# Attention, a bilinear layer and a SoLU layer in one kernel: single-bank tiles for the products of h, other room for the first raw words of w_in, a fence behind block 4's first casts

## The chip, the cores and the metric

The kernel runs on one core of one Trainium2 chip. The metric is device microseconds (us) of one execution. The core's engines are PE (TensorE, the matrix products), DVE (VectorE), ACT (ScalarE), POOL (GpSimd) and SP (SyncE, which here only issues transfers). SBUF is the working memory; PSUM, eight banks of 512 fp32 values per partition, is where PE leaves its products.

## The reference

Three layers follow one another over 2304 tokens (4 x 576) of width 512.

```
x   = repeat(attention over 4-token means) + local attention (|i - j| < 4)   # 8 heads of 64
x   = ((x @ w_a) * (x @ w_b)) @ w_out                                        # 512 -> 1536 -> 512
h   = x @ w_in                                                               # 512 -> 1024
e   = exp(h - max(h));  solu = h * e / (sum(e) + 1e-9)
out = ((solu - mean) / sqrt(var + 1e-6) * g_ln) @ w_out2                     # 1024 -> 512
```

## The kernel before, in words

The values are fp32. A product is made of three PE products of a high and a low part (hi x hi, hi x lo, lo x hi), so each operand is split: ACT casts the high part, DVE or POOL subtracts it to get the low part. The weights arrive as raw 64-bit words; `w_stages` loads one (`load`, L102), has ACT scale its two halves (`s1`, L112 and L113), DVE shift and add them (`s2`, `s3`), ACT cast the high part (`s4`) and DVE or POOL form the low part (`s5`).

**First part.** Attention, and the bilinear layer in blocks of 512 tokens; block 4, the last, has 256. A block goes in 12 chunks j: `emit_A` (L655) makes a and b, `emit_a` copies a out (ACT), `emit_mult` multiplies (DVE, L668), `emit_p` splits the product (ACT ph L674, POOL pl L675), and `emit_B` (L696) adds the chunk to four sums, one or two chunks later. At j = 11 the sums are copied out (o1, L704 and L709) and stored to DRAM. The first weights lie in 36 slots `w0` to `w35`, three for each chunk; a slot is free when its chunk in block 4 is done, and is then used again. `slot(31)` held o1 of block 4.

**Passage.** During block 4 `start_p2` (called at j = 2) closes the attention's pools, opens those of the last stage and lists the work on w_in and w_out2 (16 pieces) in `w2q`, each item with the chunk from which it may be traced. Every raw word goes into the slot that its weight will have, so a load waits for the slot's old weight.

**Last part.** Tokens in 18 tiles of 128. The first four go singly: `emit_C1` multiplies a tile with w_in into h (L815), a tile of two PSUM banks with two buffers, and DVE reduces it to its row maximum (L818). From there the tiles go in pairs p = 2 to 8 through `emit_C` (L835): seven products of 6 matmuls each stand for eight, with sums of operands (S1 to S4, made by POOL in `x_sums`, split by ACT in `x_hi` and by POOL in `x_lo`) and of weights (T1 to T4). Their four targets d, a, b, c are the halves of two such h tiles. ACT copies a to v1 (L845), DVE makes u2 = b + v1 (L848) and u3 = c + u2 (L852), and `top` adds and takes the maximum in one operation (L839); h ends in SBUF, in slots 31 and 34. The order on PE is d, a, b, c, a again, b again, d again.
For each tile follow the SoLU and the norm: `emit_exp` (ACT, L870), `emit_mean` (DVE, L875 and L877), `emit_sq` (ACT), `emit_V` (DVE transposes, then a store), `emit_raw` (loads it back with rows and columns exchanged), `emit_rs` (L888 to L893), `emit_T` (ACT L920, POOL L922), and `emit_D` (L931), 24 matmuls with w_out2; `emit_out` scales and stores. A pair's `emit_D` comes two pairs after its `emit_C`. `x_load` reads a pair's o1 into slots 20 and 23, of which there is one set; `x_hi` of pair 2 casts into slots 26 and 29, `x_lo` of pair 2 fills 32 and 35.

**What sets the order.** The program is written in one order; a planner then orders each engine's instructions, by that order and its own estimates of durations, and puts in the waits. A tile is given on when all its readers are done. `pin` ties an engine's instructions to the order as written: all engines in block 0, PE in blocks 1 and 2, four engines in block 3, all engines from pair 3 on. `pin(())`, in block 4, for the four single tiles and for pair 2, ties nothing.

Of the kernel before, what the change touches and what calls it, by code (L numbers as in the profile page):

```python
# [7 lines left out]
F32 = mybir.dt.float32  # L8
# [34 lines left out]
def kernel(  # L43
# [15 lines left out]
):  # L59
    nc = tc.nc  # L60
    PE, ACT, DVE, POOL, SP = nc.tensor, nc.scalar, nc.vector, nc.gpsimd, nc.sync
    last = {}
    done = [0]

    def pin(engines=None):

        traced = nc.cur_bb.bb.instructions
        for ins in traced[done[0]:]:
            if ins.engine in last and (engines is None or ins.engine in engines):
                tc.add_manual_dep(  # L70
                    ins, last[ins.engine].name,
                    mybir.DependencyInfo(mybir.DependencyClass.NoSync, mybir.DependencyReason.DATA), reason="pin")
            last[ins.engine] = ins
        done[0] = len(traced)
# [19 lines left out]
    def slot(n, dt=F32R, shape=(128, 2, 512), name=None):  # L94
        return base.tile(list(shape), dt, tag=f"w{n}", name=name or f"w{n}")

    def w_stages(src, i, dst, at, gcol=None, lo_eng=DVE, keep=None):


        st = {}  # L100

        def load():  # L102
            raw = slot(at, I32, (128, 1024), "raw")
            SP.dma_start(out=raw, in_=src[i])
            words = raw.rearrange("p (a b) -> p a b", b=2)
            st["low"], st["high"] = words[:, :, 0], words[:, :, 1]

        def s1():


            hw = f32(st["high"])
            ACT.activation(out=hw, in_=hw, func=AF.Prelu, scale=2.0 ** -112, alpha=2.0 ** 32)  # L112
            ACT.activation(out=st["low"], in_=st["low"].bitcast(U32), func=AF.Copy, scale=2.0 ** -29)  # L113

        def s2():
            st["w"] = base.tile([128, 512], I32, tag="wm", bufs=3, name="wm")
            DVE.tensor_scalar(out=st["w"], in0=st["high"], scalar1=3, scalar2=None, op0=ALU.logical_shift_left)

        def s3():
            DVE.tensor_tensor(out=st["w"], in0=st["w"], in1=st["low"], op=ALU.add)  # L120
            if keep is not None:
                keep[i] = f32(st["w"])

        def s4():
            t = slot(at)
            dst[i] = t[:, 0, :], t[:, 1, :]
            if gcol is None:
                ACT.copy(out=dst[i][0], in_=f32(st["w"]))
            else:
                ACT.activation(out=dst[i][0], in_=f32(st["w"]), func=AF.Copy, scale=gcol)  # L130

        def s5():
            hi, lo = dst[i]
# [544 lines left out]
    def emit_B(blk, j):  # L678
        w = width[blk]
        if j == 0:  # L680
            if w == WIDE:
                t = aps.tile([128, 2, 512], F32, tag="S", name="accS")
                accs[blk] = [ps.tile([128, 512], F32, tag=f"acc{n}", name=f"acc{n}") for n in range(2)] + [t[:, n] for n in range(2)]
            else:
                t = [ps.tile([128, 2, 256], F32, tag=f"acc{n}", name=f"acc{n}") for n in range(2)]
                accs[blk] = [t[n // 2][:, n % 2, :] for n in range(4)]
        def store(m):
            SP.dma_start(out=o1d[blk][:, :, 128 * m:128 * m + 128].rearrange("i p t -> p i t"),
                         in_=o1s[blk][:, m, 0:w].rearrange("p (i t) -> p i t", t=128))

        ph, pl = pt.pop((blk, j))
        wh, wl = W1[3 * j + 2]
        for m in range(4):
            ms = slice(m * 128, m * 128 + 128)
            for i, (wt, x) in enumerate(((wh, ph), (wh, pl), (wl, ph))):
                PE.matmul(out=accs[blk][m], lhsT=wt[:, ms], rhs=x,  # L696
                          start=(j == 0 and i == 0 and (w == WIDE or m % 2 == 0)), stop=(j == NCH - 1 and i == 2),
                          skip_group_check=True)
            if j == NCH - 1:
                if m == 0:  # L700
                    o1s[blk] = (base.tile([128, NP, WIDE], F32, tag="xs", name="o1") if w == WIDE else
                                slot(31, F32, (128, NP, 256), "o1"))
                if m < 2 or w < WIDE:
                    ACT.copy(out=o1s[blk][:, m, 0:w], in_=accs[blk][m])  # L704
                    store(m)
        if j == NCH - 1 and w == WIDE:

            for m in (2, 3):
                DVE.tensor_copy(out=o1s[blk][:, m, 0:w], in_=accs[blk][m])  # L709
                store(m)  # L710
# [90 lines left out]

        return first, second, [split(n) for n in range(4)]

    def h_of():
        return p2["ps"].tile([128, FF2], F32, tag="h", bufs=2, name="h")

    def emit_C1(i):
        hi, lo = x1.pop(("t", i))
        h = h_of()
        for n in range(2):  # L810
            for k in range(4):
                wh, wl = W2[2 * k + n]
                ks = slice(k * 128, k * 128 + 128)
                for q_, (x, w) in enumerate(((hi, wh), (hi, wl), (lo, wh))):
                    PE.matmul(out=h[:, n * 512:n * 512 + 512], lhsT=x[:, ks], rhs=w,  # L815
                              start=(k == 0 and q_ == 0), stop=(k == 3 and q_ == 2))
        mx = col("mx")
        DVE.tensor_reduce(out=mx, in_=h, axis=AX.X, op=ALU.max)  # L818
        hst[i] = {"h": h, "mx": mx}

    def emit_C(p):


        ops = x1.pop(p)
        sb = p2["sb"]
        d, a, b, c = (t[:, 512 * n:512 * n + 512] for t in (h_of(), h_of()) for n in range(2))
        i, k = 2 * p, 2 * p + 1

        def prod(out, x, b, more=False):
            xh, xl = ops[x]  # L830
            for kt in range(2):
                wh, wl = WB[b, kt]
                ks = slice(kt * 128, kt * 128 + 128)
                for q_, (xx, w) in enumerate(((xh, wh), (xh, wl), (xl, wh))):
                    PE.matmul(out=out, lhsT=xx[:, ks], rhs=w, start=(kt == 0 and q_ == 0 and not more),  # L835
                              stop=(kt == 1 and q_ == 2), skip_group_check=True)

        def top(out, in0, in1, op, init, mx):
            DVE.tensor_tensor_reduce(out=out, in0=in0, in1=in1, scale=1.0, scalar=init, op0=op, op1=ALU.max, accum_out=mx)  # L839

        hA, hB = (slot(n, F32, (128, FF2), "h") for n in (31, 34))
        prod(d, "S1", "T1")
# [182 lines left out]
    def start_p2():  # L1025
        open_p2()
        load_o1(0)
        load_o1(1)
        stages = [w_stages(w2, i, W2, 3 * (i // 2) + i % 2, g_sb[:, i - 8:i - 7] if i >= 8 else None,
                           POOL if i % 2 else DVE, wk) for i in range(16)]  # L1030
        for n, i in enumerate((0, 1, 5, 4, 2, 3, 7, 6) + tuple(range(8, 16))):
            kt = n // 4
            w2q.append((max(2, n // 2), stages[i][0]))
            body = list(stages[i][1:])
            if n in (2, 6):
                ts = []
                body.insert(3, lambda kt=kt, ts=ts: (ts.extend(t_sums(kt)), ts[0]()))
            if n in (3, 7):
                body.insert(3, lambda ts=ts: ts[1]())
            w2q.extend((min(max(3, n // 2 + 1) + m // 2, 11), f) for m, f in enumerate(body))  # L1040
            if n in (3, 7):
                w2q.extend((7 if kt == 0 else 11.5, lambda ts=ts, q_=q_: ts[2][q_]()) for q_ in range(4))
        w2q.append((11.2, lambda: x_load(2)))
        w2q.sort(key=lambda x: x[0])

# [49 lines left out]
    blk = NBLK - 1  # L1095
    advance(1e9)
    for j in range(NCH):
        if j == 2:
            start_p2()
        for n in range(2):  # L1100
            emit_A(blk, j, n, 0, width[blk])
            (emit_mult if n else emit_a)(blk, j)
        emit_p(blk, j)
        prev.append((blk, j))
        if len(prev) > 2 or j < 1:
            emit_B(*prev.pop(0))
        for t_, f in w2q:
            if j <= t_ < j + 1:
                f()
        if j == 8:  # L1110
            split_o1(0)
            split_o1(1)
            load_o1(2)
            load_o1(3)
        pin(())
    for x in prev:
        emit_B(*x)

# [6 lines left out]
    for i in range(4):  # L1125
        emit_C1(i)
        emit_exp(i)
        emit_mean(i)
        emit_sq(i)
        emit_V(i)  # L1130
        emit_rs(i)
        emit_raw(i)
        if i < 2:
            split_o1(i + 2)
        if i == 1:
            x_sums(2)
            x_hi(2)
            x_lo(2)
            x_load(3)
        if i == 3:  # L1140
            x_sums(3)
            x_hi(3)
            x_lo(3)
        if i == 2:
            emit_D(0)
            emit_out(0)
        if 1 <= i < 3:
            emit_T(i - 1)
# [114 lines left out]
```

## Time and profile before

| | |
|---|---|
| runs shown | 786.82, 782.67, 786.75 us; median 786.75 |
| profiled execution | 783.57 us, of which the span of the instructions is 781.8 |
| PE | 745.9 us busy (95%), 4648 matmuls |
| DVE, ACT, POOL | 455.6 (58%), 329.0 (42%), 267.5 (34%) |
| mean granted clock of TensorE | 0.983 of 2.4 GHz |
| chain that ended last | PE 78%, DVE 12%, ACT 5%, issue 2%, DMA 1% |

Busy time is summed over the span and says nothing of where an engine was idle; that is seen in the stretches and waits below. A matmul's time in the trace overlaps with its neighbours': the time from one start to the next is what it costs. A row of a timeline with x6 merges six instructions. Matmul records can be missing. Block 4 begins at about 505 us, pair 2 at 591, and the last PE work ends 4 us before the span does.

### The profile page before, as it was taken

The page shows a single profiled execution, that of the slowest core. Times are in us where ns is not written, and L with a number is a line of the kernel's source. Part 1 is how long each engine was busy: PE and PEld are TensorE (multiplying, and loading weights), DVE is VectorE, ACT ScalarE, POOL GpSimd, SP SyncE. Part 2 cuts the span into 40 slices and gives each one's busy share as a digit, 9 for nine tenths or more (in the row PEclk, how much of TensorE's full clock was granted, in tenths as well). Part 3 has the DMA queues.
Part 4 walks back from the last instruction along what each step waited for, and adds up shares of the span by engine and source line. Part 5 has one row for each costly group of instructions (what it writes and reads, how often), then busy time and mean ns, then how long its engine had stood idle before and what let it go on. Part 6 is the DMA issues. An engine that isn't in the chain of part 4 may idle for free.

```text
span 781.8 us, 12401 instructions
## 1 busy us (share of the span) xinstructions
PE 745.9 (95%) x4648; PEld 606.0 (78%) x4648; DVE 455.6 (58%) x880; ACT 329.0 (42%) x700; POOL 267.5 (34%) x269
## 2 busy tenths in 40 slices
PE   8989999999999999999999999999979599999997
PEld 7777767777777777777788888898968377777786
DVE  6579779884422434422337868336997665556550
ACT  4558677653222223222221111277555425444441
POOL 2200110123333332332211111136568836767332
PEclk9799999999999999999999999999999989999999
DMA  8992875245232315321102120195116254444431
GB/s 244 247 386 83 261 242 187 60 148 154 81 100 82 108 31 148 96 86 46 57 18 84 34 63 18 55 289 196 55 61 195 69 160 145 153 161 135 134 128 62
DMA packets 79669, 98.88 MB, mean 126 GB/s; under 512 B 10457, under 2 KB 60473, under 8 KB 79609
## 3 DMA queue, kind: packets, MB, share of 16 engines
q1 hardware_dynamic: 79064, 97.88, 40.2%
q8 instruction: 36, 0.59, 0.3%
q10 hardware_dynamic: 544, 0.21, 0.1%
q14 instruction: 25, 0.20, 0.1%
HBM read 73.95 MB, written 24.12 MB: 125 GB/s over the span
## 4 chain that ended last, share of the span: by engine, by line
PE 78%; DVE 12%; ACT 5%; issue 2%; DMA 1%; SPq 0%; POOL 0%; ACTq 0%; DVEq 0%; POOLq 0%
PE ab L655 32%; PE o L931 11%; PE acc L696 9%; PE h L835 7%; PE accS L696 7%; PE pv L320 3%; PE h L815 2%; PE lo L505 2%; DVE wm L120 2%; DMA raw<-w 1%; PE lS L396 1%; PE lS L172 1%; DVE u L875 1%; PE S L258 1%; PE PT L303 1%
## 5 line engine op out<-in xcount | busy, mean ns | idle before, releaser
L655 PE MATMUL ab<-xTh,w 128*128 128x512 f32 (+1 forms) x976 | 292.2, 371 | 3.1 <-DVE a L668 1.5
L655 PEld LDWEIGHTS ab<-xTh,w 128*128 128x128 f32 x976 | 177.0, 188 | 39.5 <-issue 3.3
L655 PE MATMUL ab<-xTl,w 128*128 128x512 f32 (+1 forms) x488 | 179.2, 367 | 0.6 <-DVE xTl L539 0.6
L675 POOL TENSOR_TENSOR pl<-a,ph 128x512 fp32r<-128x512 f32 (+1 forms) x48 | 61.1, 1272 | 172.4 <-ACT ph L674 172.2
L655 PEld LDWEIGHTS ab<-xTl,w 128*128 128x128 f32 x488 | 92.0, 188 | 15.5 <-DVE xTl L539 1.0
L668 DVE TENSOR_TENSOR a<-a,ab 128x512 f32<-128x512 f32 (+1 forms) x60 | 37.8, 630 | 100.1 <-PE ab L655 93.7
L696 PE MATMUL acc<-ph,w 128*128 128x512 f32 (+1 forms) x288 | 89.5, 363 | 0.0
L663 ACT COPY a<-ab 128x512 f32<-128x512 f32 (+1 forms) x60 | 32.5, 542 | 103.9 <-PE ab L655 101.1
L242 POOL TENSOR_TENSOR vp<-vp 72x256 f32<-72x256 f32 x24 | 20.4, 862 | 147.5 <-DMA vp<-vp 147.5
L674 ACT CAST ph<-a 128x512 fp32r<-128x512 f32 (+1 forms) x60 | 34.7, 578 | 85.9 <-DVE a L668 85.9
L696 PE MATMUL accS<-ph,w 128*128 128x512 f32 x192 | 67.0, 390 | 0.0
L696 PEld LDWEIGHTS acc<-ph,w 128*128 128x128 f32 x288 | 52.3, 190 | 9.4 <-issue 1.4
L931 PE MATMUL o<-w,cTh 128*128 128x512 f32 x192 | 59.2, 389 | 0.0
L696 PE MATMUL acc<-pl,w 128*128 128x512 f32 (+1 forms) x144 | 51.4, 359 | 2.6 <-POOL pl L675 2.6
L922 POOL TENSOR_TENSOR cTl<-raw,cTh 128x512 fp32r<-128x512 f32 x24 | 34.0, 1439 | 23.6 <-ACT cTh L920 23.6
L696 PEld LDWEIGHTS accS<-ph,w 128*128 128x128 f32 x192 | 36.0, 188 | 7.7
L931 PEld LDWEIGHTS o<-w,cTh 128*128 128x128 f32 x192 | 36.0, 188 | 7.5
L120 DVE CUSTOM_DVE_ANT_0 wm<-raw,wm 128x1024 uint16<-128x1024 uint16 x52 | 38.7, 749 | 1.9
L112 ACT ACTIVATE raw<-raw 128x512 f32<-128x512 f32 x52 | 35.7, 687 | 7.8 <-DMA raw<-w 7.7
L696 PE MATMUL accS<-pl,w 128*128 128x512 f32 x96 | 37.5, 390 | 0.0
L931 PE MATMUL o<-w,cTl 128*128 128x512 f32 x96 | 37.4, 389 | 0.0
L281 ACT ACTIVATE E<-S,pm 72x144 f32<-72x144 f32 x64 | 23.3, 372 | 32.4 <-DVE pm L269 22.7
(161 smaller groups left out, 1299.3 us busy)
## 6 DMA issues: line engine op xcount, KB each, us to landing
raw<-w SPq DMA_DIRECT2D x52, 512.0 KB
qkr<-qkp SPq DMA_DIRECT2D x32, 288.0 KB
vd<-v SPq DMA_DIRECT2D x18, 512.0 KB
raw<-vd SPq DMA_DIRECT2D x72, 128.0 KB
vp<-vp SPq DMA_DIRECT2D x16, 288.0 KB
pd<-lT SPq DMA_DIRECT2D x12, 384.0 KB
out<-ob SPq DMA_DIRECT2D x18, 256.0 KB
vw<-vwin SPq DMA_DIRECT2D x32, 140.0 KB
```

The lines of the kernel that those rows point to most:

```text
L112: ACT.activation(out=hw, in_=hw, func=AF.Prelu, scale=2.0 ** -112, alpha=2.0 ** 32)
L120: DVE.tensor_tensor(out=st["w"], in0=st["w"], in1=st["low"], op=ALU.add)
L320: PE.matmul(out=st["pv"][e * 64:e * 64 + 64, :], lhsT=vt[:, e * 64:e * 64 + 64], rhs=st["PTs"][:, e, n * 2 // len(v), :], start=(n == 0), ...
L655: PE.matmul(out=abs_[blk, j][n][:, c0:c1], lhsT=w[:, ws], rhs=x[:, k, c0:c1], start=(k == 0 and i == 0), stop=(k == 3 and i == 2), skip_gr ...
L663: ACT.copy(out=a, in_=abs_[blk, j][0])
L668: DVE.tensor_tensor(out=a, in0=a, in1=pb, op=ALU.mult)
L674: ACT.copy(out=ph, in_=a)
L675: (POOL if blk else DVE).tensor_tensor(out=pl, in0=a, in1=f32(ph), op=ALU.subtract)
L696: PE.matmul(out=accs[blk][m], lhsT=wt[:, ms], rhs=x, start=(j == 0 and i == 0 and (w == WIDE or m % 2 == 0)), stop=(j == NCH - 1 and i == ...
L835: PE.matmul(out=out, lhsT=xx[:, ks], rhs=w, start=(kt == 0 and q_ == 0 and not more), stop=(kt == 1 and q_ == 2), skip_group_check=True)
L922: POOL.tensor_tensor(out=h4(lo)[:, k], in0=raw[:, k], in1=f32(h4(hi)[:, k]), op=ALU.subtract)
L931: PE.matmul(out=o, lhsT=x[:, k, :], rhs=w, start=(k == 0 and q_ == 0), stop=(k == 7 and q_ == 2))
```

## The change

In `emit_C1` and `emit_C` the h tiles of two banks become four tiles of one bank each, c0 to c3 (`bank`). `emit_C1` no longer leaves h in PSUM: for each half DVE adds zeros to it and writes it to SBUF (slots 31 and 34) with its running maximum, by `top`, which is now shared. o1 of block 4 moves from slot 31 to slot 26. `start_p2` is called at j = 0; the first six raw words of w_in in its order go into the tiles cTh0, cTl0, cTh1, cTl1 and u of the last stage, may be loaded from j = 0 on, and the list of times of the casts is another. In block 4's first two chunks ACT, DVE and POOL are pinned, and the last instruction of each there becomes its `fence`, behind which all that is traced later on that engine has to stay where nothing else pins it. `emit_D(0)` is written after the fourth single tile instead of the third.

```diff
     def pin(engines=None):
 ...
-            if ins.engine in last and (engines is None or ins.engine in engines):
+            free = engines is not None and ins.engine not in engines
+            before = (fence if free else last).get(ins.engine)
+            if before is not None:
...
-            raw = slot(at, I32, (128, 1024), "raw")
+            raw = raw_of() if raw_of else slot(at, I32, (128, 1024), "raw")
...
-                                slot(31, F32, (128, NP, 256), "o1"))
+                                slot(26, F32, (128, NP, 256), "o1"))
...
-    def h_of():
-        return p2["ps"].tile([128, FF2], F32, tag="h", bufs=2, name="h")
+    def bank(n):
+        return p2["ps"].tile([128, 512], F32, tag=f"c{n}", name="c")
+
+    def top(out, in0, in1, op, init, mx):
+        DVE.tensor_tensor_reduce(out=out, in0=in0, in1=in1, scale=1.0, scalar=init, op0=op, op1=ALU.max, accum_out=mx)
...
-        h = h_of()
+        h = slot(31 + 3 * (i % 2), F32, (128, FF2), "h")
+        m = [col("m1", 1), col("mx")]
         for n in range(2):
+            t = bank(2 * (i % 2) + n)
...
-        DVE.tensor_reduce(out=mx, in_=h, axis=AX.X, op=ALU.max)
+            top(v(h[:, 512 * n:512 * n + 512]), v(t), zz.unsqueeze(1).to_broadcast([128, 4, 128]), ALU.add,
+                m[0] if n else -3.0e38, m[n])
...
-        d, a, b, c = (t[:, 512 * n:512 * n + 512] for t in (h_of(), h_of()) for n in range(2))
+        d, a, b, c = (bank(n) for n in (3, 0, 1, 2))
...
+        order = (0, 1, 5, 4, 2, 3, 7, 6) + tuple(range(8, 16))
+        room = {order[n]: (lambda t=t, b=b: p2["sb"].tile([128, 1024], I32, tag=t, bufs=b, name="raw"))
+                for n, (t, b) in enumerate((("cTh0", 1), ("cTl0", 1), ("cTh1", 1), ("cTl1", 1), ("u", 2), ("u", 2)))}
...
-            w2q.append((max(2, n // 2), stages[i][0]))
+            w2q.append((0 if n < 6 else max(2, n // 2), stages[i][0]))
...
-            w2q.extend((min(max(3, n // 2 + 1) + m // 2, 11), f) for m, f in enumerate(body))
+            w2q.extend((min((1, 1, 2, 2, 3, 3, 5, 5, 5, 5, 6, 6, 7, 7, 8, 8)[n] + m // 2, 11), f) for m, f in enumerate(body))
...
-                w2q.extend((7 if kt == 0 else 11.5, lambda ts=ts, q_=q_: ts[2][q_]()) for q_ in range(4))
+                w2q.extend((5 if kt == 0 else 11.5, lambda ts=ts, q_=q_: ts[2][q_]()) for q_ in range(4))
...
-        if j == 2:
+        if j == 0:
             start_p2()
...
-        pin(())
+        pin((ACT.engine, DVE.engine, POOL.engine) if j < 2 else ())
+        if j < 2:
+            fence.update({e.engine: last[e.engine] for e in (ACT, DVE, POOL)})
...
-        if i == 2:
+        if i == 3:
             emit_D(0)
             emit_out(0)
```

## Rows read from the trace of the kernel before

**Rows 1.** Stretches: us, busy time of each engine (instructions), granted clock, DMA share, GB/s

```profile
535.00:567.00 32.00, 32.00 (x238) 30.16 (x238) 24.20 (x35) 20.50 (x40) 17.81 (x17) 1.00 0.32 99
567.00:591.00 24.00, 19.84 (x94) 16.66 (x94) 21.40 (x41) 13.07 (x24) 15.61 (x12) 0.93 0.30 94
591.00:615.00 24.00, 21.38 (x93) 16.97 (x93) 14.30 (x25) 11.03 (x17) 20.72 (x20) 1.00 0.53 170
615.00:635.00 20.00, 12.42 (x43) 9.64 (x42) 12.18 (x29) 7.43 (x12) 10.10 (x10) 0.74 0.42 132
635.00:745.00 110.00, 105.30 (x453) 83.87 (x452) 67.78 (x146) 50.73 (x78) 68.52 (x62) 1.00 0.42 134
```

**Rows 2.** Waits from 505 to 745 us: us in total, times, longest

```profile
PE h L835 <- DVE u L848: 12.0, 6, 7.6
...
ACT raw L112 <- DMA raw<-w: 6.6, 6, 2.2
...
PE acc L696 <- POOL pl L675: 2.6, 2, 2.1
...
PE h L815 <- DVE ss L888: 2.0, 1, 2.0
...
PE h L835 <- ACT h L855: 1.8, 1, 1.8
...
PE h L835 <- DVE u L852: 0.8, 1, 0.8
```

**Rows 3.** Timeline of PE, pair 4 and pair 8: start, us, instruction, idle before

```profile
650.72 1.66 PE L835 MATMUL h<-tw,xo 128*128 128x512 f32 x6 [0.85 <-DVE u L848]
652.22 1.53 PE L835 MATMUL h<-w,xo 128*128 128x512 f32 x6
653.58 1.52 PE L835 MATMUL h<-tw,xo 128*128 128x512 f32 x6
...
738.61 1.65 PE L835 MATMUL h<-tw,xo 128*128 128x512 f32 x6 [0.85 <-DVE u L848]
```

**Rows 4.** Timeline of DVE and ACT, pair 4

```profile
649.98 0.69 DVE L848 TENSOR_TENSOR u<-h,v 128x512 f32<-128x512 f32 x1 [3.08 <-PE h L835]
...
654.51 0.59 ACT L855 COPY h<-h 128x512 f32<-128x512 f32 x1 [4.80 <-DVE m L839]
```

**Rows 5.** Timeline of PE, pair 3 and the D behind it

```profile
626.27 1.22 PE L835 MATMUL h<-tw,xTh 128*128 128x512 f32 x2 [7.58 <-DVE u L848]
...
629.00 1.05 PE L835 MATMUL h<-w,xTh 128*128 128x512 f32 x2
...
634.75 5.60 PE L931 MATMUL o<-w,cT 128*128 128x512 f32 x24
640.19 0.62 PE L931 MATMUL o<-w,cTh 128*128 128x512 f32 x2
```

**Rows 6.** Timeline of DVE: single tiles and the first pair

```profile
572.30 1.21 DVE L818 TENSOR_REDUCE mx<-h 128x1 f32<-128x1024 f32 x1
...
598.92 1.22 DVE L875 SCALAR_TENSOR_TENSOR u<-h,u 128x1024 f32<-128x1024 f32 x1 [2.82 <-ACT u L870]
...
609.43 0.69 DVE L839 CUSTOM_DVE_ANT_0 h<-h,u 128x512 f32<-128x512 f32 x1
...
618.85 2.20 DVE L875 SCALAR_TENSOR_TENSOR u<-h,u 128x1024 f32<-128x1024 f32 x1
```

**Rows 7.** Timelines: end of block 4, operands of pair 2, v1 of pair 3

```profile
574.09 0.41 DVE L668 TENSOR_TENSOR a<-a,ab 128x256 f32<-128x256 f32 x1
...
576.98 0.72 POOL L675 TENSOR_TENSOR pl<-a,ph 128x256 fp32r<-128x256 f32 x1
...
589.09 0.28 PE L696 MATMUL acc<-ph,w 128*128 128x256 f32 x1
...
589.46 2.00 POOL L768 TENSOR_TENSOR xo<-xr,xo 128x512 fp32r<-128x512 f32 x2 [2.06 <-PE acc L696]
...
591.31 0.37 ACT L704 COPY o<-acc 128x256 f32<-128x256 f32 x1
...
622.40 0.58 ACT L845 COPY v<-h 128x512 f32<-128x512 f32 x1
```

More of the change, by code (lines that the diff above doesn't have):

```diff
@@ L61 @@
     PE, ACT, DVE, POOL, SP = nc.tensor, nc.scalar, nc.vector, nc.gpsimd, nc.sync
-    last = {}
+    last, fence = {}, {}
     done = [0]
@@ L68, in pin @@
         for ins in traced[done[0]:]:
-            if ins.engine in last and (engines is None or ins.engine in engines):
+            free = engines is not None and ins.engine not in engines
+            before = (fence if free else last).get(ins.engine)
+            if before is not None:
                 tc.add_manual_dep(
-                    ins, last[ins.engine].name,
+                    ins, before.name,
                     mybir.DependencyInfo(mybir.DependencyClass.NoSync, mybir.DependencyReason.DATA), reason="pin")
@@ L95, in slot, with w_stages @@
         return base.tile(list(shape), dt, tag=f"w{n}", name=name or f"w{n}")
-    def w_stages(src, i, dst, at, gcol=None, lo_eng=DVE, keep=None):
+    def w_stages(src, i, dst, at, gcol=None, lo_eng=DVE, keep=None, raw_of=None):
         st = {}
         def load():
-            raw = slot(at, I32, (128, 1024), "raw")
+            raw = raw_of() if raw_of else slot(at, I32, (128, 1024), "raw")
             SP.dma_start(out=raw, in_=src[i])
@@ L814, in emit_C1 @@
                 for q_, (x, w) in enumerate(((hi, wh), (hi, wl), (lo, wh))):
-                    PE.matmul(out=h[:, n * 512:n * 512 + 512], lhsT=x[:, ks], rhs=w,
-                              start=(k == 0 and q_ == 0), stop=(k == 3 and q_ == 2))
-        mx = col("mx")
-        DVE.tensor_reduce(out=mx, in_=h, axis=AX.X, op=ALU.max)
-        hst[i] = {"h": h, "mx": mx}
+                    PE.matmul(out=t, lhsT=x[:, ks], rhs=w, start=(k == 0 and q_ == 0), stop=(k == 3 and q_ == 2))
+            v = lambda x: x.rearrange("p (a b) -> p a b", b=128)
+            top(v(h[:, 512 * n:512 * n + 512]), v(t), zz.unsqueeze(1).to_broadcast([128, 4, 128]), ALU.add,
+                m[0] if n else -3.0e38, m[n])
+        hst[i] = {"h": h, "mx": m[1]}
     def emit_C(p):
@@ L836, in prod @@
                               stop=(kt == 1 and q_ == 2), skip_group_check=True)
-        def top(out, in0, in1, op, init, mx):
-            DVE.tensor_tensor_reduce(out=out, in0=in0, in1=in1, scale=1.0, scalar=init, op0=op, op1=ALU.max, accum_out=mx)
         hA, hB = (slot(n, F32, (128, FF2), "h") for n in (31, 34))
@@ L1028, in start_p2 @@
         load_o1(1)
+        order = (0, 1, 5, 4, 2, 3, 7, 6) + tuple(range(8, 16))
+        room = {order[n]: (lambda t=t, b=b: p2["sb"].tile([128, 1024], I32, tag=t, bufs=b, name="raw"))
+                for n, (t, b) in enumerate((("cTh0", 1), ("cTl0", 1), ("cTh1", 1), ("cTl1", 1), ("u", 2), ("u", 2)))}
         stages = [w_stages(w2, i, W2, 3 * (i // 2) + i % 2, g_sb[:, i - 8:i - 7] if i >= 8 else None,
-                           POOL if i % 2 else DVE, wk) for i in range(16)]
-        for n, i in enumerate((0, 1, 5, 4, 2, 3, 7, 6) + tuple(range(8, 16))):
+                           POOL if i % 2 else DVE, wk, room.get(i)) for i in range(16)]
+        for n, i in enumerate(order):
             kt = n // 4
-            w2q.append((max(2, n // 2), stages[i][0]))
+            w2q.append((0 if n < 6 else max(2, n // 2), stages[i][0]))
             body = list(stages[i][1:])
```

## The prediction

> **What bounds the kernel now.** I read the busy time by stage first [rows 1], the waits second [rows 2], and then timelines of single stretches. In [rows 1] the reader sees two regimes. From 635 to 745 us, the steady run of pairs, PE is busy 105.30 of 110 us and no other engine above 68.5: PE sets the pace, and what PE loses there moves the end one for one. From 567 to 635 us, the passage from block 4 to the pairs, PE is busy 19.84 of 24, 21.38 of 24 and 12.42 of 20: 14.4 us idle, and its granted clock falls to 0.93 and 0.74. So there are two places to look: many small losses per pair, and one large hole.
>
> [Rows 2] names them. In the pairs PE waits for DVE's u2 (L848) 12.0 us in 6 waits, one of them 7.6; the five others are 0.9 each. The 7.6 is the large hole, before pair 3. The rest of the passage: 2.0 for the first tiles' SoLU (L815, put down to ss L888), 1.8 for the copy of h (L855), 0.8 for u3 (L852), 2.6 for block 4's pl.
>
> **The change, part by part.** *Four tiles of one bank, in emit_C.* Today d and a are the halves of one two-bank tile, b and c those of another. The fourth product goes to c and needs nothing of u2 = b + v1, yet in [rows 3] it starts at 650.72 right after u2 has read b (649.98 + 0.69 = 650.67 in [rows 4]). That is the shared tile: a write into one half waits for a read of the other. The seventh product, into d, waits in the same way for ACT's copy of a (654.51 in [rows 4]), and ACT's copy for DVE's read of d. With a tile for each bank these three go. What stays is real: the fifth product needs v1 (long copied), the sixth needs u2, a product (1.36) and a half away; the seventh needs d's first read, which ends about 1.9 after c is done (0.69 for u3, 0.69 for the top, two hand-overs) while the fifth and sixth product take 2.72. So nothing is late next by about 0.8 us.
> The price, from [rows 3]: a product is 653.58 - 652.22 = 1.36, a D is 640.19 - 634.75 = 5.44 [rows 5], so a pair is 7 x 1.36 + 2 x 5.44 = 20.40 us of PE. Four pairs took 738.61 - 650.72 = 87.89, or 21.97 each. The difference, 1.57, is the two waits and the restart after each. Pairs 4 to 8 pay it: 5 x 1.57 = **7.9 us off**. POOL has the next load, 68.52 of 110, or 13.7 a pair, and fits into 20.4. After pair 8 PE runs D without a break, so it all reaches the end. From the other side the gain is bounded by 4.4 (five waits of 0.9 alone).
> Pair 2 pays 0.8 and 1.8 of its own [rows 2]; these lie ahead of a chain treated below, and I don't count them twice.
>
> *The same tiles in emit_C1.* Each half of h is copied by DVE into SBUF, with its maximum, and its bank is free. Today the third tile's products wait for the first tile's L875, the 2.0 of [rows 2]; now only for two copies. Cost on DVE: one reduction of 1.21 goes, two tops of 0.69 come (that of u3 + d has the same shape) plus two short reads: some 0.3 each, 1.3 over four tiles [rows 6]. The SoLU of these tiles now reads h from SBUF. In [rows 6] L875 took 1.22 with h in PSUM while POOL worked, and 2.20 with h in SBUF beside POOL: between 0 and 1.0 more each, 0 to 4 us on DVE in a stretch where DVE is busy 21.4 of 24 [rows 1]. I take 1.5.
> The Trainium skill has a rule on this (SBUF — State Buffer, section SBUF: two separate sides): DVE and GpSimd share one pair of ports as an exclusive lock, and a DVE instruction with two SBUF inputs waits for a GpSimd instruction that holds it. The two rows of L875 agree. By the rule every one of the four would be at risk of a whole POOL instruction, which gives 4 us on DVE and not on PE; the sum is then 1 to 2 us worse.
>
> *The first six raws of w_in.* They no longer wait for block 4's first weights to be used up, and land before block 4. Today ACT stood 6.6 us in six waits for raws [rows 2]. The loads move ahead on SP's queue by two chunks; what they pass there is block 3's four stores and the loads behind them, and the loads have only freed memory to wait for, so I cost the passing at 0 to 1 us. Their casts do not begin earlier: the fence holds ACT, DVE and POOL until block 4's first two chunks are cast. What is queued behind the fence is only w_in's and later work, not PE. Gain: casts that run together instead of at the pace of the loads, 0 to 5 us on DVE's backlog; from 535 to 567 DVE was busy 24.2 of 32 [rows 1], so it had holes before it had its jam.
>
> *o1 of block 4 in slot 26, not 31.* This speaks against the change. Slot 26 is where pair 2's operands (x_hi) are cast to. They were cast at leisure during block 4; now they wait until block 4's last sums are copied and stored. Call E the end of block 4's last product, 589.4 today (589.09 + 0.28 in [rows 7]). Then: last copy out, E + 2.3 (591.31 + 0.37); store, estimated as 2.2, the longest wait for a raw in [rows 2]; cast, two of 0.59, 1.2; four POOL subtractions, two of which took 2.00 [rows 7], 4.0. Pair 2's operands are ready at E + 9.7. Today they were ready at 591.46, E + 2.1. So this path gets 7.6 us longer.
> Pair 3 hangs on it through POOL and the single xr buffers: from 591.46 to ACT's v1 of pair 3, at 622.40 [rows 7], I count 30.9 us, nearly without a hole on POOL (20.72 of 24 busy from 591 to 615, [rows 1]). From v1 pair 3 ends after 0.6, three products (4.1) and a hand-over, 4.9. So pair 3 would end at E + 45.5; today at 634.75 = E + 45.4. In other words the path through slot 26 eats what the free banks give pair 2 and 3 (the 7.6 wait and its slow clock: the first product behind it took 626.27 to about 629 instead of 1.36, [rows 5]), and **what is gained in the passage is what E gains**.
>
> *E.* Block 4's last multiplication ran at 574.09, behind a jam of casts and one reduction on DVE; its pl was ready at 576.98 + 0.72 = 577.7 [rows 7]. Its twelve products take about 1.5, so 579.2 was possible, but PE had them ordered among the first tiles' products until 589.4. Now the first tiles' order has no wait in it, DVE's jam is thinner by up to 5 and thicker by about 1.5. Bounds: 574 and 589.4; I take 580, nearest to what was ready. *emit_D(0) behind tile 3* costs nothing: the 24 products are the same and fill PE while pair 2 waits for its operands.
>
> **Sum.** The profiled execution took 783.57 us. 783.57 - 7.9 (pairs) - 9.2 (E from 589.2, where the passage neither gains nor loses, to 580) = 766.5. The three runs shown have a median of 786.75, two near 786.8 and one at 782.67, and the profiled one belongs to the lower; I add 1.5 for a median of such a mixture: **768 us**.
>
> **The rivals.**
> *A, block 4 ends when it did* (E = 589.4, the order on PE stays): only the pairs gain. 783.57 - 7.9 + 0.2 + 1.5 = 777. For it: the order is settled by a planner's estimates, not by what was ready. Against: the 2.0 wait in the middle is gone.
> *B, the passage packs*: E at 575, and the path to pair 3 loses 4 of its 30.9: 783.57 - 7.9 - 14.2 - 4 + 1.5 = 759. For it: 14.4 us of idle PE. Against: POOL's load there.
> *C, the waits in the pairs are not the shared tile's*: then they stay, and with an E near 585 the time is 781; with E unchanged 785, no change. Against: the same pattern in each pair to 0.1 us.
> *D, slower*: PE takes block 4's last products behind the first tiles and D(0), since these no longer wait for anything; then slot 26 holds pair 2 while nothing is left to fill PE. By the sum it is slower by more than 0.5% when E is later than 601, 11.6 us after today's. Two products of D and a tile (5.44 + 5.4) put ahead of it do nearly that; E = 603 gives 791. Against: block 4 comes first in the program.
>
> **Chances.** Forecast (E from 575 to 586, 763 to 774) 0.50; A 0.20; B 0.14; C 0.08; D 0.08. The range 757 to 780 holds the forecast, A and most of B; it leaves out C and D and the far side of B, about 0.2. A measurement of this kernel tells about 0.5% (3.9 us) from no change: faster than that 0.84 (forecast, A, B), within 0.08 (most of C), slower 0.08 (D).
>
> **What would show it.** The pairs: period from 21.97 to about 20.4, and no wait of PE for L848. First tiles: no wait at L815 for SoLU, L818 gone, two custom operations in place of each. Slot 26: pair 2's casts (L761) right behind block 4's stores, pair 2's first product within 10 us of E. E itself: block 4's last L696 before 586. I am wrong if the period stays at 21.9, or if pair 3 ends much off E + 45.5 (then another path than POOL's and the xr buffers' binds), or if PE stands idle in block 4 behind the fence.

## The result, and the profile after

The changed kernel takes 776.69 us (median of 12 runs, 773.84 to 780.90) against 784.61 (12 runs, 779.98 to 787.10) of the kernel before: ratio 0.9904 [0.9877, 0.9931]. That is 7.9 us, all of it in the pairs. The 9.2 us expected of the passage did not come. The profiled execution took 780.9 us (span 779.1). Line numbers are 2 to 7 higher than before.

The stretches of [rows 1], after: us, busy time of each engine (instructions), granted clock, DMA share, GB/s.

```profile
535.00:567.00 32.00, 30.73 (x219) 28.72 (x218) 23.64 (x34) 21.41 (x40) 16.62 (x15) 1.00 0.41 135
567.00:591.00 24.00, 20.51 (x137) 18.66 (x136) 21.70 (x41) 11.19 (x21) 12.68 (x13) 1.00 0.10 34
591.00:615.00 24.00, 23.28 (x105) 18.64 (x105) 18.13 (x37) 13.42 (x22) 16.72 (x16) 1.00 0.62 197
615.00:635.00 20.00, 10.35 (x41) 7.90 (x40) 12.63 (x28) 9.89 (x15) 17.30 (x18) 0.84 0.44 135
635.00:745.00 110.00, 110.00 (x479) 90.87 (x478) 73.97 (x155) 53.40 (x82) 67.92 (x62) 0.98 0.44 141
```

The last row is the gain: TensorE has no idle time left in the pairs (110.00 of 110, before 105.30). The four rows above it hold 15.1 us of idle TensorE, before 14.4: the passage gained nothing. The waits, to read against [rows 2]:

```profile
PE c L842 <- ACT v L849: 7.3, 1, 7.3
...
PE ab L657 <- ACT a L665: 4.4, 2, 3.5
...
ACT raw L114 <- DMA raw<-w: 3.2, 4, 1.2
...
PE ab L657 <- DVE a L670: 2.9, 4, 1.0
...
PE c L842 <- DVE mx L810: 2.4, 1, 2.4
```

The waits for u2 are gone, in the pairs and ahead of pair 3. But pair 3 now waits 7.3 us for ScalarE's v1, block 4 waits 7.3 us in six waits for its own a-copies and multiplications (L665, L670), and pair 3's first product waits 2.4 for VectorE's maximum of pair 2 (L810).

The timeline of TensorE, pair 4 and pair 8, to read against [rows 3]:

```profile
650.78 1.52 PE L842 MATMUL c<-tw,xo 128*128 128x512 f32 x6
652.14 1.52 PE L842 MATMUL c<-w,xo 128*128 128x512 f32 x6
653.50 2.88 PE L842 MATMUL c<-tw,xo 128*128 128x512 f32 x12
...
732.38 1.52 PE L842 MATMUL c<-tw,xo 128*128 128x512 f32 x6
```

The rows begin with a pair's first product, those of [rows 3] with its fourth. Products follow each other without a hole, and four pairs take 732.38 - 650.78 = 81.60, or 20.40 each.

The passage, to read against [rows 5] and [rows 7]: timelines of the block's end, of pair 2's operands, and of v1 and pair 3.

```profile
580.40 2.45 PE L822 MATMUL c<-w,o1w 128*128 128x512 f32 x10
...
582.70 0.28 PE L657 MATMUL ab<-xTh,w 128*128 128x256 f32 x1
...
585.83 0.38 DVE L670 TENSOR_TENSOR a<-a,ab 128x256 f32<-128x256 f32 x1
...
586.78 0.74 POOL L677 TENSOR_TENSOR pl<-a,ph 128x256 fp32r<-128x256 f32 x1 [5.73 <-ACT ph L676]
...
594.31 1.05 ACT L924 CAST cTh<-raw 128x1024 fp32r<-128x1024 f32 x1 [1.65 <-DMA raw<-vd]
595.26 0.64 ACT L706 COPY o<-acc 128x256 f32<-128x256 f32 x2
...
596.84 0.28 PE L698 MATMUL acc<-ph,w 128*128 128x256 f32 x1
...
597.74 0.36 ACT L706 COPY o<-acc 128x256 f32<-128x256 f32 x1
...
603.83 2.64 POOL L770 TENSOR_TENSOR xo<-xr,xo 128x512 fp32r<-128x512 f32 x2 [0.85 <-ACT xo L763]
...
622.58 0.39 PE L842 MATMUL c<-w,xTl 128*128 128x512 f32 x1
...
625.87 2.56 POOL L743 TENSOR_TENSOR xr<-xr 128x256 f32<-128x256 f32 x3 [2.20 <-DMA xr<-o1d]
...
631.59 0.83 ACT L763 CAST xo<-xr 128x768 fp32r<-128x768 f32 x1 [1.23 <-POOL xr L743]
632.33 0.58 ACT L849 COPY v<-c 128x512 f32<-128x512 f32 x1
...
632.96 1.22 PE L842 MATMUL c<-w,xTh 128*128 128x512 f32 x2 [7.27 <-ACT v L849]
...
635.68 1.06 PE L842 MATMUL c<-tw,xTh 128*128 128x512 f32 x2
...
639.88 2.46 PE L935 MATMUL o<-w,cT 128*128 128x512 f32 x10
```

Block 4's last ab products start at 582.70, behind ten products of the first tiles; its last multiplication runs at 585.83, and its last product ends at 597.12, the E of the prediction. The last row is where pair 3 has ended. Above it, v1 runs right behind the second cast of x_hi of pair 4, which waits for GpSimd's sums. The product that v1 copies had ended at 622.97 (622.58 + 0.39), 9.4 us earlier. Hold on to that pair of rows.

Executions differ by up to 9 us in where block 0 begins (last section), so from here on times are counted from block 4's first product (505.50 before, 509.19 after), and the passage is the time from there to pair 4's first product. In the two profiles, start to block 4 is 3.7 us longer after, the passage 1.5 longer, pairs 4 to 8 and the rest 7.8 shorter: 777.39 - 774.76 = 2.6 between the ends of the last product.

### The profile page after: what moved, and what is told of

Read it like the earlier page. It is cut to its first block, busy times and chain, and to the rows that moved or that the text cites. A ratio compares the mean times of both kernels' runs of the same rounds, so it can differ in the third digit from the quotient of the medians.

```text
span 779.1 us, 12416 instructions
## 1 busy us (share of the span) xinstructions
PE 742.8 (95%) x4648; PEld 605.5 (78%) x4648; DVE 463.8 (60%) x892; ACT 329.8 (42%) x700; POOL 259.6 (33%) x269
## 4 chain that ended last, share of the span: by engine, by line
PE 72%; DVE 13%; ACT 4%; DMA 4%; issue 4%; POOL 2%; SPq 1%; DVEq 0%; ACTq 0%; POOLq 0%
PE ab L657 31%; PE o L935 11%; PE acc L698 8%; PE c L842 7%; PE accS L698 7%; PE pv L322 3%; DVE wm L122 3%; DVE wm L119 2%; PE lo L507 2%; PE lS L398 1%; DVE w L137 1%; DMA raw<-vd 1%; DVE a L670 1%; PE S L260 1%; DMA vd<-v 1%
## 5 line engine op out<-in xcount | busy, mean ns | idle before, releaser
L677 POOL TENSOR_TENSOR pl<-a,ph 128x512 fp32r<-128x512 f32 (+1 forms) x48 | 58.3, 1215 | 184.6 <-ACT ph L676 184.6
L670 DVE TENSOR_TENSOR a<-a,ab 128x512 f32<-128x512 f32 (+1 forms) x60 | 37.8, 629 | 103.7 <-PE ab L657 100.3
L665 ACT COPY a<-ab 128x512 f32<-128x512 f32 (+1 forms) x60 | 32.6, 543 | 107.1 <-PE ab L657 104.3
L244 POOL TENSOR_TENSOR vp<-vp 72x256 f32<-72x256 f32 x24 | 18.7, 794 | 149.0 <-DMA vp<-vp 149.0
L122 DVE CUSTOM_DVE_ANT_0 wm<-raw,wm 128x1024 uint16<-128x1024 uint16 x52 | 42.5, 821 | 1.7
L283 ACT ACTIVATE E<-S,pm 72x144 f32<-72x144 f32 x64 | 23.3, 372 | 32.9 <-DVE pm L271 30.9
```

Of the source, the lines that this page charges most:

```text
L665: ACT.copy(out=a, in_=abs_[blk, j][0])
L670: DVE.tensor_tensor(out=a, in0=a, in1=pb, op=ALU.mult)
L677: (POOL if blk else DVE).tensor_tensor(out=pl, in0=a, in1=f32(ph), op=ALU.subtract)
```

## The experiments

Each ratio is against runs of the kernel before on the same chip. The columns in us are from one profiled execution each.

| run | ratio [95%] | last multiplication of block 4 | E | pair 4 starts |
|---|---|---|---|---|
| before | 1 | 68.6 | 83.9 | 140.1 |
| changed | 0.9904 [0.9877, 0.9931] | 76.6 | 87.9 | 141.6 |
| e1_C_two_bank | 1.0005 [0.9979, 1.0030] | 76.9 | 88.1 | 143.5 |
| e2_banks_in_C | 0.9863 [0.9819, 0.9908] | 68.0 | 84.9 | 139.3 |
| e3_no_fence | 0.9898 [0.9851, 0.9945] | 70.5 | 79.7 | 135.2 |
| e4_banks_only | 0.9829 [0.9783, 0.9875] | 74.3 | 86.4 | 138.8 |
| e5_o1_in_ob | 0.9842 [0.9811, 0.9874] | 76.8 | 90.1 | 137.5 |
| e6_Bcopy | 0.9888 [0.9841, 0.9936] | 76.6 | 83.0 | 138.6 |
| e7_ob_Bcopy | 0.9885 [0.9821, 0.9949] | 76.8 | 86.4 | 135.3 |
| e8_banks_ob_Bcopy | 0.9838 [0.9796, 0.9881] | 72.9 | 82.7 | 136.4 |
| e9_old_times | 0.9883 [0.9845, 0.9921] | 76.7 | 86.1 | 140.9 |
| e10_PE_order | 0.9936 [0.9906, 0.9966] | 69.7 | 73.9 | 143.8 |
| e11_old_times_ob_Bcopy | 0.9856 [0.9816, 0.9896] | 78.1 | 83.7 | 141.3 |
| e12_PE_order_ob_Bcopy | 0.9952 [0.9917, 0.9988] | 69.0 | 73.7 | 145.2 |
| e13_no_low | 0.9796 [0.9766, 0.9826] | 66.8 | 79.3 | 136.0 |
| e14_no_low_ob | 0.9825 [0.9784, 0.9865] | 68.8 | 80.8 | 138.0 |
| e15_banks_ob | 0.9790 [0.9763, 0.9816] | 74.5 | 88.0 | 135.4 |
| e16_ob_D0 | 0.9855 [0.9825, 0.9885] | 78.9 | 92.2 | 140.6 |
| e17_v1_first | 0.9823 [0.9783, 0.9864] | 77.5 | 89.6 | 134.2 |
| e18_best | 0.9771 [0.9739, 0.9803] | 73.4 | 85.3 | 129.1 |

### The parts of the change alone

*e1: emit_C back to halves of two-bank tiles.*

```diff
-        d, a, b, c = (bank(n) for n in (3, 0, 1, 2))
+        d, a, b, c = (t[:, 512 * n:512 * n + 512] for t in (h_of(), h_of()) for n in range(2))
```

> The changed kernel, but in emit_C the four products share two tiles of two banks again, as before (the pool of PSUM tiles is closed after the four single tiles and opened anew; emit_C1 keeps its single banks). Theory 'shared tile': the period of a pair goes back from the changed kernel's to 21.9 us, PE waits again for L848, and the kernel loses all that the change brought, 7 to 9 us: 784 to 786, ratio to before 0.998 to 1.003. Rival 'the waits were of the data': nothing changes, ratio 0.990.

*e2: the kernel before with that line the other way round, and nothing else.*

> The kernel before, with one-bank tiles in emit_C alone (the PSUM pool closed and opened anew after the single tiles); no other part of the change. Theory 'the pairs alone paid': period 20.4, and at least the whole gain of the change, ratio 0.988 to 0.991; pair 2, freed of its own two waits of 0.8 and 1.8, may bring 1 to 3 us more (0.985). Rival 'the passage of the changed kernel gains and something else loses': the ratio is 0.995 or above.

Waits of TensorE in e1:

```profile
PE h L846 <- DVE u L856: 13.3, 6, 8.8
```

With the halves the six waits for u2 are back, the period is 21.9 and the whole gain is gone (1.0005); with one-bank tiles alone the period is 20.4. The step on the pairs stands, and the rest of the change together earns nothing measurable.

*e3: the fence and the pins of block 4's first two chunks taken out; e4: raw words, casts and pins as before, the rest of the change kept.*

```diff
-        pin((ACT.engine, DVE.engine, POOL.engine) if j < 2 else ())
-        if j < 2:
-            fence.update({e.engine: last[e.engine] for e in (ACT, DVE, POOL)})
+        pin(())
```

> The changed kernel without the fence and without the pins of block 4's first two chunks (order free there, as before). Theory 'pins at the start of block 4' (they hold the second chunk's copy of a behind two copies of o1, 3.4 us): from the first product of block 4 to its last, E, 87.9 us in the changed kernel and 83.7 before, falls to 83 to 84, and the kernel gains 3 to 4 us on the changed one: ratio 0.985. Rival 'DVE's run of casts sets E' (25 us without a hole in both kernels): E stays within 1 us of 87.9 and the ratio at 0.990. Third: with the raws there early the planner puts casts ahead of block 4's copies, and E is later, ratio 0.995.

> The changed kernel with its tiles of one bank, slot 26 and the later D(0), but the first six raws, start_p2, the times of the casts and the pins as before. Theory 'pins at the start': E falls to 83 to 84 us after block 4's start, ratio 0.985 to 0.987. Theory 'early raws do help, the rest costs': E rises to 90 and the ratio to 0.994. Theory 'slot 26 and the copies of o1 set the passage': E and the ratio stay as in the changed kernel, 87 to 89 us and 0.990.

Without the fence the casts go ahead of block 3's last copy: TensorE waits 6.0 us there, block 4 begins 8 us later, and that cancels its shorter passage. Without raw words and fence pair 4 starts 2.8 us earlier than in the changed kernel. The two other such pairs of runs, e15 against e5 and e8 against e7, give 2.1 earlier and 1.1 later. In the times the kernels with early raw words and fence are the slower ones in all three pairs, by 0.0075, 0.0052 and 0.0047 of the ratio (4 to 6 us); only in the first pair do the intervals stay apart. So these parts gain nothing and probably cost a few us, of which the profiles of the passage show at most 2.8.

### Slot 26, and E

*e5: block 4's o1 in two buffers that are free then, instead of slot 26.*

```diff
-                                slot(26, F32, (128, NP, 256), "o1"))
+                        t = [p2["sb"].tile([128, 512], F32, tag="ob", bufs=2, name="o1") for _ in range(2)]
```

> The changed kernel, but block 4's four o1 tiles lie in the two output buffers of the last stage instead of slot 26, so pair 2's x_hi no longer waits for block 4's o1 stores; all else as in the changed kernel. Theory (the path through slot 26 sets when pair 3 ends, 42.8 us after the end E of block 4's last product): x_hi of pair 2 can be cast as soon as its operands are there, 5 to 7 us earlier; v1 of pair 3 is no longer the last to come to pair 3's products of h; pair 3 ends at E+35 to E+40, the time falls by 3 to 8 us against the changed kernel (ratio to the kernel before 0.981 to 0.986). Rival (the vector work between C(2) and pair 3 is as late by itself): pair 3 ends at E+42 to E+43 again, and the ratio stays at 0.990.

*e6: in block 4 the four last sums first, then their copies to SBUF. e7: both edits. e8: both on e4.*

> The changed kernel, but in block 4 all four of the last products' sums are issued before the first of their copies to SBUF, so a product in the same bank no longer waits between two copies. Theory (E is late because the last twelve products are split by copies that stand behind a cast waiting for a DMA): the products of the last chunk run in one piece, E falls by 6 to 8 us (549.5 to 542-543 after the first product of block 0), pair 3 ends 4 to 8 us earlier, ratio 0.980 to 0.985. Rival (ScalarE and VectorE are behind with the a-copies and multiplies of chunks 9 to 11, and the copies only show it): E falls by 2 at most, ratio 0.988 to 0.991; the stores of o1 leave later by the same order, so it can also lose 1 or 2 us.

> Both edits on the changed kernel: o1 of block 4 in the two output buffers, and the four sums ahead of their copies. If E and the path through slot 26 stand one behind the other, their gains add up: pair 3 ends 8 to 14 us earlier and the ratio is 0.972 to 0.980. If a common third cause (the casts of the raw words of w_in on VectorE and ScalarE beside block 4) sets both, it is no better than the better of the two alone, 0.984 to 0.990.

> The same two edits on the kernel that has only the one-bank tiles of the change (raw words of w_in issued and cast as in the kernel before, no fence): ratio 0.983 without the edits. If the early raw words and the fence help once the two waits are gone, this stays 4 us or more behind the run with all of it (0.978 to 0.983 against 0.972 to 0.980); if they bring nothing or cost something, this is the fastest, at 0.970 to 0.977.

Slot 26 costs 4.1 us (141.6 to 137.5), as its theory had it. In e6 E came 4.9 us earlier and pair 4 3.0; the time can't be told from the changed kernel's. Both together give 6.3 in the profile, and no more than e5 in the time. The gains that the theories of e6 and e7 forecast, and both ranges of e8, were missed: the ratios came out higher. E is not the whole of it.

*e9: the casts of w_in at the places of the kernel before. e11: the same with both edits of e7.*

> The changed kernel with one thing of the change undone: the casts of w_in's raw words stand in the program where the kernel before has them (two to three chunks of block 4 later); the early raw words, the fence, the tiles, slot 26 and D(0) stay. Theory (block 4 ends late because these casts now come ahead of its own copies and multiplications on ScalarE and VectorE: its last multiplication stands 76.6 us after block 4's first product, 68.6 in the kernel before): the last multiplication falls back to 68 to 71, its plane pl to 72 to 74, and E falls from 87.9 to 82 to 85; pair 3 ends 2 to 5 us earlier, ratio to the kernel before 0.984 to 0.988. Rival (the pins of the first two chunks, by which its copies lag 3 to 5 us from the start, delay the rest by themselves): the last multiplication stays at 74 or later and the ratio at 0.990.

> The kernel with both edits (o1 of block 4 in the two output buffers, four sums ahead of their copies) and the casts of w_in back at the places of the kernel before, with raw words early and the fence. If the casts ahead of block 4's work are what it still loses, the last multiplication falls from 76.8 to 68-72 and pair 3's successor starts at 131 to 134 after block 4's first product instead of 135.3; ratio 0.974 to 0.981. If the total work between block 4's start and pair 3 on VectorE and GpSimd sets it, the order changes nothing: 135 to 138 and 0.982 to 0.988.

The last multiplication did not move (76.7): the casts' due places do not make block 4 late. e11 missed both its ranges for the passage: pair 4 starts at 141.3, 6.0 us later than in e7, while the time can't be told from e7's.

*e10: e6 with a fence on TensorE behind block 4's last product. e12: e7 with it.*

```diff
     for x in prev:
         emit_B(*x)
+    pin((PE.engine,))
+    fence[PE.engine] = last[PE.engine]
```

> The kernel with the four sums ahead of their copies, and in addition a fence on TensorE: no product of the first tiles goes ahead of block 4's last product. E is then given by what is ready (the last plane at 78.3 us after block 4's first product) plus 1.5 to 3: 80 to 82, against 83.0. The prediction's step (what E gains, pair 3 gains, by the path through slot 26 that is 42.8 us long): pair 3 ends 1 to 3 us earlier, at 123 to 127 after block 4's first product against 127.9. Rival (TensorE has as much to do either way, and what it stands idle before E is lost at the end): TensorE stands idle 3 to 6 us more ahead of E, and pair 3 ends at 127 to 131; ratio 0.988 to 0.993.

> Both edits and the fence on TensorE. Without slot 26's path E no longer sets pair 2's operands, so by the theory the fence is worth nothing here and costs what TensorE stands idle ahead of E: pair 4 starts at 135 to 140 after block 4's first product against 135.3, ratio 0.984 to 0.990. Rival (an early E also frees VectorE and ScalarE sooner for the first tiles): 131 to 134, ratio 0.976 to 0.982.

The timeline of TensorE in e10, at block 4's last product:

```profile
580.34 0.28 PE L698 MATMUL acc<-ph,w 128*128 128x256 f32 x1
580.46 17.42 PE L830 MATMUL c<-w,o1w 128*128 128x512 f32 x76
597.71 1.52 PE L850 MATMUL c<-w,xo 128*128 128x512 f32 x6
```

This decides on E. Order alone, of the sums (e6) and of TensorE (the fence), brings the last multiplication from 76.6 to 69.7 and E to 73.9: the prediction's 580 was 74.5 on this scale (580 - 505.50), so E is where it was forecast, to 0.6 us. And pair 4 starts 2.2 us *later* than in the changed kernel and 5.2 later than in e6; in e12 it starts 9.9 later than in e7. The rows show why: the 96 products of the first tiles, of which 77 to 96 were done ahead of E elsewhere, now lie behind it (76 of them in the second row), and ahead of E TensorE stands idle where they were (8.7 us in six waits for L670).

*e13: the addition of the low words of w_in left out (16 instructions on VectorE). e14: the same on e5.*

```diff
-            DVE.tensor_tensor(out=st["w"], in0=st["w"], in1=st["low"], op=ALU.add)
+            if src is not w2:
+                DVE.tensor_tensor(out=st["w"], in0=st["w"], in1=st["low"], op=ALU.add)
```

> The changed kernel without the addition of the low words of w_in (VectorE's L122, about 1.07 us each, 16 of them: the weights of the last stage lose their low bits). VectorE has about 17 us less to do beside block 4; TensorE, the stores and the order of the program stay. Theory (VectorE's queue, in which block 4's multiplications stand behind these casts, sets when block 4 and the first tiles are done): the last multiplication of block 4 falls from 76.6 us after block 4's first product to 66 to 72, TensorE stands idle 3 to 8 us less, pair 4 starts at 133 to 139 instead of 141.6, ratio to the kernel before 0.980 to 0.986. Rival (order, latencies and the stores set it, and VectorE's load is beside the point): pair 4 at 140 to 142 and 0.989 to 0.991.

> The same on the kernel with o1 of block 4 in the two output buffers (pair 4 started at 137.5, ratio 0.984). Theory: VectorE's load is what is left, so pair 4 starts at 129 to 134, ratio 0.973 to 0.980. Rival: 136 to 138 and 0.982 to 0.986.

With less on VectorE, block 4's last multiplication comes 9.8 us earlier, E 8.6, pair 4 5.6. So VectorE's load does bear on E, and here, with slot 26, the passage is shorter too. The relief is not alone, though: the planner's order on TensorE changed with it (39 products of the first tiles ahead of block 4's last ab product, 58 in the changed kernel). Without slot 26 (e14) the same relief gives nothing: E is 9.3 us earlier than in e5, and pair 4 starts 0.5 later. What is left there, on ScalarE's timeline ahead of pair 3:

```profile
618.05 1.06 ACT L892 ACTIVATE sq<-u 128x1024 f32<-128x1024 f32 x1 [5.60 <-DVE u L886]
...
619.11 0.81 ACT L768 CAST xo<-xr 128x768 fp32r<-128x768 f32 x1
619.83 0.58 ACT L854 COPY v<-c 128x512 f32<-128x512 f32 x1
```

TensorE had stood since 610.7, waiting 9.8 us for this v1. Its product was done; the copy stood in ScalarE's queue behind a square of pair 2 and x_hi of pair 4.

*e15: e4 with e5's buffers. e16: e5 with the first D behind tile 2.*

> A version to keep: the one-bank tiles, o1 of block 4 in the two output buffers, raw words and casts of w_in as in the kernel before, no fence, sums and copies as in the changed kernel. With the tiles alone the ratio was 0.983, with everything and the output buffers 0.984. If the wait on slot 26 is worth 4 us here too, 0.977 to 0.981; if the passage's length is set by VectorE's load, which this does not touch, 0.981 to 0.985.

> The changed kernel with o1 of block 4 in the two output buffers and with the first D behind tile 2 as in the kernel before. By the prediction this place costs nothing either way: 0.983 to 0.986, as with the output buffers alone. Rival (D(0) behind tile 3 is what TensorE has left to fill the wait of pair 3): 2 to 4 us slower than that, 0.986 to 0.990.

e15 has the lowest ratio so far, and slot 26 was worth 3.4 us of passage there too. e16 can't be told from e5 in the time; its profile has pair 4 3.1 us later, so D(0) behind tile 3 costs nothing, as predicted.

### v1's place in the queue

*e17: the changed kernel with x_hi, x_lo of pair 4 and rs of pair 2 behind pair 3's v1. e18: the same on e15.*

```diff
         ACT.copy(out=v1, in_=a)
+        if then:
+            then()
...
-            emit_C(p)
+            emit_C(p, late if p == 3 else None)
...
-        for i in new:
+        for i in new if p != 2 else ():
             emit_rs(i)
             emit_raw(i)
```

Here late is x_hi(4) and x_lo(4); the rs and raw left out at p = 2 follow behind emit_C(3), and so do x_load and x_sums of pair 5.

> The changed kernel, but pair 4's x_hi and x_lo and pair 2's last scalars (rs, and the loads behind them) are put behind pair 3's v1 and first sums instead of ahead of them; the work is the same. Theory (v1 of pair 3 stands behind x_hi of pair 4 on ScalarE's queue, and the path through slot 26 reaches pair 3 only by that): TensorE's wait ahead of pair 3 falls from 7.3 us to 1 to 4, pair 4 starts at 134 to 138 after block 4's first product instead of 141.6 though E stays at 87 to 88, ratio 0.981 to 0.986. Rival (pair 4 or 5 then waits for the x_hi that now come later): what pair 3 gains is lost at pair 4, and the ratio stays at 0.988 to 0.991.

> The same order on the version with the one-bank tiles, o1 of block 4 in the two output buffers and the raw words as in the kernel before (0.979). Theory: TensorE's wait of 6.6 us ahead of pair 3 falls to 1 to 4, pair 4 starts at 130 to 133 instead of 135.4, ratio 0.972 to 0.977, faster than both kernels. Rival (another wait takes its place within 2 us, or pair 4 pays): 0.977 to 0.981.

Timelines of e17, ScalarE and then TensorE:

```profile
620.70 0.59 ACT L849 COPY v<-c 128x512 f32<-128x512 f32 x1 [0.52 <-PE c L842]
...
624.75 1.05 ACT L763 CAST xo<-xr 128x1024 fp32r<-128x1024 f32 x1
...
626.94 0.84 ACT L763 CAST xo<-xr 128x768 fp32r<-128x768 f32 x1
...
627.02 0.73 PE L842 MATMUL c<-tw,xTh 128*128 128x512 f32 x2 [2.28 <-DVE u L854]
```

Waits of TensorE in e18:

```profile
PE acc L698 <- POOL pl L677: 2.8, 3, 1.8
PE ab L657 <- DVE a L670: 2.8, 2, 2.3
PE c L846 <- DVE u L858: 2.3, 1, 2.3
PE c L846 <- ACT v L853: 0.3, 1, 0.3
```

v1 now waits for its product alone, and TensorE 2.3 us for u2 instead of 7.3 for v1. Pair 4 starts 7.4 us earlier than in the changed kernel although E came 1.7 later: here the passage hung on this place, not on E. About 5.0 of the 7.4 are the shorter wait. Most of the rest is the clock: behind the 7.3 us in which TensorE stood, its granted clock was 0.50 (1.2 GHz) from 632.96 to 638.25 in the changed kernel, a product took 2.72 (632.96 to 635.68), and pair 3's last three products 6.92 instead of 3 x 1.36 = 4.08; in e17, behind 2.3 us, the clock stayed at 1.00. With this order e18 takes 765.76 us (median of 6) against 782.66, 0.9771 [0.9739, 0.9803], below both kernels' intervals. Against e15 pair 4 starts 6.3 us earlier in the profile, but the two ratios (0.9771 and 0.9790) can't be told apart, and the 0.972 to 0.977 of the theory was just missed.

## Why the prediction was right and wrong

*Right: the pairs.* 7.9 forecast, 7.8 measured; the period is 20.40 to the hundredth, e1 and e2 show that the shared two-bank tile was the cause. It is the whole gain, and the time is rival A's 777. A's reason, that the order on TensorE is settled by the planner and not by what was ready, holds. That A's number fits is in part luck: A left E where it was, but E came 4.0 us later in block 4's time and the path behind it got 2.7 shorter.

*Right: the path through slot 26.* Pair 2's operands were ready at 603.83 + 2.64 = 606.47, E + 9.4 (forecast E + 9.7). From there to v1 it took 25.9 us instead of 30.9, and pair 3 ended at E + 42.8 instead of E + 45.5. From v1 to that end the forecast had 4.9; it took 7.6, at the low clock. e5 gives the price of the path where it binds: 4.1.

*Wrong: "I take 580, nearest to what was ready".* This is the step that failed, the -9.2. In block 4's own time E was forecast at 74.5 and came at 87.9. The reason given was that the first tiles' order had lost its wait and VectorE's jam would thin. What the runs show is the reverse: E came 13.4 us behind its forecast, the shorter path behind it gave 2.7 back, and the passage, put at -9.2, measured +1.5.

Of the 13.4, 8.0 are the last multiplication (68.6 to 76.6). Products that no longer wait are put *ahead*: of the 96 products of the first tiles 58 stand ahead of block 4's last ab product in the changed kernel's order, 35 before. e2, with the first tiles as before, has 35 and the last multiplication at 68.0; e4, with their new tiles but without early raw words and fence, has 58 and 74.3; e10, by order alone, has none and 69.7. How the 8 us divide between this order and VectorE's queue stays open, since in e13 both changed. The other 5.4 lie between the last multiplication and E, 11.3 us instead of the forecast's 5.9: ScalarE's copies of block 4's sums stood behind the cast of cTh, which waited for a transfer (594.31 and 595.26 in the rows of the passage), and the sums that followed waited for the copies. e6, with the sums ahead of the copies, takes 4.9 off E.

*Wrong beneath it: "what is gained in the passage is what E gains".* e10 reached the forecast E and gained nothing, nor did e14's 9.3 us; e17 left E and gained 7.4. The forecast treated E as a release, where it was a place in TensorE's order: work not done ahead of it is done behind it. And the chain of 30.9 us to v1 was read as one of data. Its last link was only order. In the kernel before as well, v1 (622.40 in [rows 7]) ran behind the cast of x_hi of pair 4, 5.1 us after its product was done, and u2 behind two transposes, while TensorE stood for 7.6 us [rows 5]. Timelines of the kernel before, of TensorE, ScalarE and VectorE:

```profile
616.95 0.39 PE L835 MATMUL h<-w,xTl 128*128 128x512 f32 x1
...
621.66 0.83 ACT L761 CAST xo<-xr 128x768 fp32r<-128x768 f32 x1 [3.19 <-POOL xr L741]
...
623.15 2.35 DVE L899 STREAM_TRANSPOSE v<-u 128x1024 f32<-128x1024 f32 x2
```

Had the rows above v1 and u2 been read, the hole would have been priced by that cast and those transposes.

*Small terms.* The SoLU with h in SBUF was put at 1.5 us; its four runs took 1.22, 1.27, 1.22 and 1.23, so nothing. ScalarE's waits for raw words fell from 6.6 to 3.2, and the runs with and without early raw words show no gain from it; why is not shown. "PE stands idle in block 4 behind the fence" had been named as what would show the forecast wrong: it is there (3.3 us of idle in the first 28 of block 4, before 2.0).

## What to carry to other kernels

When a wait goes, ask what the planner will put into the hole: work that is free to run early is run early, at the cost of the block whose end you count on. Where a stage's end is held by one short instruction, look at the row ahead of it on its engine before following its data: a cheap gain here (7.4 us of the passage) was to move two casts, and the work around them, behind a copy whose product had been done for 9.4 us. And give each accumulating product that is read on its own a PSUM tile of its own.

## What had not been expected of the hardware

The head of the kernel differs between executions, and its granted clock with it. Stretches ahead of block 0, first the changed kernel, then e14, whose order is the same there:

```profile
24.00:32.00 8.00, 4.93 (x90) 4.27 (x87) 6.76 (x16) 2.58 (x6) 1.91 (x2) 0.95 0.96 244
32.00:40.00 8.00, 7.85 (x60) 6.55 (x58) 0.00 (x0) 3.82 (x8) 0.77 (x2) 0.50 0.97 247
```

```profile
24.00:32.00 8.00, 7.62 (x138) 6.77 (x139) 5.96 (x14) 6.09 (x14) 2.25 (x2) 1.00 1.03 325
32.00:40.00 8.00, 5.58 (x83) 4.59 (x79) 5.75 (x10) 6.83 (x15) 3.10 (x4) 1.00 1.05 218
```

In the changed kernel TensorE stood for more than 3 us between 24 and 32, then ran at 0.50 (1.2 GHz); block 0's first product came at 47.65. In e14 the clock stayed at 1.00, and it came at 38.62. Of the 20 profiles the eight at 1.00 over the first 48 us have it at 38.6 to 41.6, the six at 0.82 to 0.89 at 42.2 to 47.7. The two go together, and the spread is larger than most terms of this study.

VectorE's product from SBUF shows both its durations within one pair, timelines of VectorE and GpSimd after:

```profile
642.40 1.22 DVE L879 SCALAR_TENSOR_TENSOR u<-h,u 128x1024 f32<-128x1024 f32 x1 [1.31 <-ACT u L874]
...
645.81 2.33 DVE L879 SCALAR_TENSOR_TENSOR u<-h,u 128x1024 f32<-128x1024 f32 x1
...
644.51 2.54 POOL L926 TENSOR_TENSOR cTl<-raw,cTh 128x512 fp32r<-128x512 f32 x2 [2.61 <-ACT cTh L924]
```

1.22 with GpSimd idle, 2.33 beside its subtraction. The Trainium skill (SBUF — State Buffer, section SBUF: two separate sides) has a VectorE instruction with two SBUF inputs wait for the ports while a GpSimd instruction that reads SBUF holds them. These rows agree: 1.11 us more for 1.24 us of overlap. The four of the first tiles overlapped with GpSimd by 0.4 us at most, and were spared.
